# Six row blocks turned by TensorE, lists turned two experts ahead, and a new order of stage 1, in a fused attention and expert kernel

## The chip, the cores and the metric

The kernel runs on one core of a Trainium2 chip. The metric is the time of one execution on the device in microseconds (us), lower is better. The kernel before took 283.99 us (median of three runs, 281.12 to 286.87). A core has TensorE (PE; its weight loads are listed as PEld), VectorE (DVE), ScalarE (ACT), GpSimd (POOL) and SyncE (SP), and 16 DMA engines which all DMA issues share. [...]

## The reference

```python
# q, k, v: (2 batches, 8 heads, 768 tokens, 64)
state = gamma * state + outer(k[t], v[t])       # per batch and head, gamma fixed for a head
y[t]  = scale * q[t] @ state                    # linear attention with decay
x     = y of all heads side by side             # (2, 768, 512)
logits = x @ w_gate                             # 8 experts
local  = sigmoid(x @ w_local)
e[s] = argmax(logits[s]) if s == 0 or local[s] < 0.5 else e[s-1]     # runs along the tokens
out[s] = softmax(logits[s])[e[s]] * (relu(x[s] @ w1[e[s]]) @ w2[e[s]])
```

Each of the 1536 tokens goes to one expert, `w1` is 512 x 1024 and `w2` 1024 x 512 in float32, so the weights of all eight experts are 33.6 MB.

## The kernel before

**Stage 1** is the attention, in 12 chunks of 128 tokens (6 per batch). For chunk c the rows of `k`, `v` and (for two chunks at once) `q` are loaded (`lk`, `lv`, `lq`), POOL scales `k` and `q` by powers of gamma (`dk`, `dq`, lines 370 and 361), TensorE turns them so that the head dimension is on the partitions (`tk`, `tq`, lines 426 and 399) and ACT or DVE copies the result out of PSUM (`ek`, `eq`, line 379). Then come the scores (`sc`, line 441), their causal mask on DVE (`mk`, line 446), the part of `y` from the state (`in`, line 458) and the part from the chunk itself (`re`, line 467), and the state's update (`st`, line 502; `sn` copies it out). `xh` on ACT and `xl` on DVE write `y` as the sum of two float16 tiles, `xT` (lines 476 and 480), from which the router's logits are computed (`lo`, lines 517 and 522).

**The rows.** `xT` has features on the partitions. The experts gather tokens as rows from DRAM, so each chunk's `xT` must be turned back: before, this is one DMA transpose for each chunk (`xd`, line 485), then a DMA that writes the rows to the DRAM tensor `xs` (`xs`, line 491).

**Routing** is done for groups of three chunks (`ch`, `kr`, `ke`, `tr`, `ca`, `tc`, `oh`, `co`, `pl`, `es`, `fi`, `ad`): the choice, the carried choice along the tokens by a scan, and the place of each token in its expert's list. After the first six chunks early lists of experts 0 and 1 are made from the tokens known so far (`ep`, `eg`), their rows gathered (line 655) and turned by DMA (`xx`, line 723). With them the first halves of experts 0 and 1 can be computed in stage 1: these are the 48 **fillers** `f` (per expert 16 pieces of the first product, line 750, and 8 of the second, line 809; `ra` and `rv` are ACT's and DVE's parts of the relu). When all groups are done, `rank`, `lists` and `experts` make the final lists and `ga` gathers from them.

**Weights** are loaded in pieces of 512 KB (`W`, line 151), each split into float16 high (`wh` on ACT, line 161) and low parts (`wl` on DVE, line 169). Nine staging buffers hold pieces; the split units of two experts fit at a time. Sixteen pieces (experts 0 and 1) are loaded in stage 1 and four more at its end.

**Order.** Everything in stage 1 is issued in the order of the text `ORDER`: a token such as `xd.3` calls the function for chunk 3, and each engine executes its own instructions in that order. All loads, DMA transposes and `xs` writes are issued from SP, one after another: an issue that waits holds up what stands behind it there. **Stage 2** follows: a loop over the experts computes the second halves of experts 0 and 1 and then the other six, loading weights as it goes; `transposed` (line 716) turns the gathered lists of the next expert and starts the next gather. Below, "stage 2" begins with the first product of expert 0's second half.

Of the kernel before, what the change touches and what calls it, by code (L numbers as in the profile page):

```python
# [43 lines left out]
ORDER = """
warm.10 zero lc.0 lk.0.0 lq.0.0 lk.0.1 lq.0.1 in.0 dk.0.p.0 lc.2 tk.0.t.0 dq.0.p.0 ek.0.a.0 lc.1 lv.0 dk.0.p.1
tqh.0.0.t dq.0.p.1 tk.0.x.1 eqh.0.0.v lg ek.0.a.1 lk.1 cast tqh.0.1.t eqh.0.1.v lv.1 st.0 setup sc.0 sn.0.a lk.2
dk.1.p mk.0.0 lq.2 mk.0.1 tk.1.t re.0 ek.1.a lv.2 dk.2.p sc.1 xh.0 lk.3 xl.0 dq.2.p mk.1.0 lo.0 xd.0 st.1 mk.1.1 in.1
lv.3 sn.1.a dk.3.p tq.2.0.t lk.4 re.1 eq.2.0.a xs.0 tq.2.1.t xh.1 W tk.2.x xl.1 eq.2.1.a st.2 ek.2.a dk.4.p xd.1 lo.1
sn.2.a sc.2 lq.4 in.2 wh.a mk.2.0 wh.a mk.2.1 xs.1 tk.3.t wl re.2 W ek.3.a wl dq.4.p sc.3 xh.2 W xl.2 st.3 mk.3.0 xd.2
lo.2 mk.3.1 sn.3.a wh.a in.3 lv.4 ch.0 wh.a ch.0 kr.0 wl wh.a lk.5 re.3 ke.0 ch.0 ch.0 ch.0 wh.a wl xs.2 tr.0 xh.3 wl  # L50
tq.4.0.t W tq.4.1.x ca.0 eq.4.0.a st.4 eq.4.1.a xl.3 dk.5.p tc.0 W sn.4.a tk.4.t oh.0 co.0 ek.4.a wl lo.3 xd.3 sc.4
pl.0 es.0 wh.a pl.0 lv.5 pl.0 wh.a in.4 mk.4.0 wh.a lk.6 mk.4.1 wh.a fi.0 re.4 ad.0 wl xs.3 wl lq.6 tk.5.t xh.4 wl
ek.5.a xl.4 dk.6.p sc.5 W wl lo.4 mk.5.0 W in.5 mk.5.1 dq.6.p tk.6.t xd.4 re.5 ek.6.v wh.a lv.6 wh.a wl tq.6.0.t xh.5
wl lk.7 tq.6.1.x eq.6.0.a xl.5 eq.6.1.a lo.5 wh.a xs.4 sc.6 ch.1 wh.a W ch.1 ch.1 kr.1 ch.1 wl st.6 ke.1 W ch.1 mk.6.0
dk.7.p tr.1 sn.6.a in.6 ca.1 xd.5 tk.7.t mk.6.1 wh.a tc.1 lv.7 wh.a oh.1 wl co.1 ek.7.a re.6 pl.1 es.1 lk.8 wh.a pl.1
pl.1 wh.a tot sc.7 xh.6 xs.5 ev wl W xl.6 fi.1 st.7 ad.1 ep wl lo.6 sn.7.a lq.8 in.7 wl eg.0 mk.7.0 mk.7.1 eg.1 W wh.a
wl re.7 wh.a dk.8.p xd.6 xh.7 dq.8.p xx.0.0 tk.8.t xl.7 ek.8.a lo.7 xx.1.0 wh.a wh.a wl xs.6 tq.8.0.t tq.8.1.x wl
eq.8.0.a W f eq.8.1.a wl f in.8 wl lv.8 f lk.9 f wh.a f W f wh.a wl f ra wl st.8 xd.7 rv f sn.8.a dk.9.p ra f W rv f
tk.9.t wh.a f lv.9 ek.9.a wl f wh.a f xs.7 ra wl f lk.10 rv wh.a f wh.a f wl ra lq.10 st.9 wl f rv sn.9.a sc.8 W
dk.10.p f mk.8.0 W mk.8.1 tk.10.x dq.10.p f ek.10.a lv.10 re.8 wh.a wh.a lk.11 wl sc.9 xh.8 wl wh.a lv.11 tq.10.0.x  # L60
xl.8 wh.a f mk.9.0 eq.10.0.a xd.8 lo.8 mk.9.1 in.9 ch.2 ch.2 kr.2 ch.2 ch.2 dk.11.p re.9 ke.2 xs.8 ch.2 wl xh.9 tr.2
tq.10.1.x ca.2 st.10 eq.10.1.a sc.10 xl.9 sn.10.a wl xd.9 tc.2 mk.10.0 lo.9 oh.2 in.10 mk.10.1 co.2 xs.9 re.10 pl.2
es.2 pl.2 pl.2 tk.11.x xh.10 fi.2 xl.10 ek.11.a f ad.2 xd.10 lo.10 sc.11 in.11 mk.11.0 mk.11.1 xs.10 f re.11 f xh.11
xl.11 f xd.11 lo.11 hd.0 f ch.3 f ch.3 kr.3 ch.3 f ch.3 ke.3 ch.3 tr.3 f ca.3 xs.11 ra f f rv tc.3 f oh.3 co.3 f pl.3
es.3 ra f pl.3 pl.3 tot f f rank fi.3 f ad.3 lists ra experts ga rest W prob W W ga rv rv f xx.0.1 f f W f ra f rv ga
f f f f ga f f f hd.1 ga
"""
# [954 lines left out]
```

## Time and profile before

| | |
|---|---|
| median of three runs | 283.99 us (281.12 to 286.87) |
| the profiled execution | 283.82 us, of which the span of the trace is 282.0 us |
| PE busy | 236.5 us (84%) |
| DVE, ACT, POOL busy | 160.6 us (57%), 127.2 us (45%), 63.7 us (23%) |
| DMA | 61.76 MB, mean 219 GB/s; 58156 of 80339 packets under 512 B |

The page divides the span into 40 equal slices and gives for each the busy share of every engine in tenths, TensorE's granted clock and what the DMA engines moved. A busy engine is no bound by itself: what counts is which wait ends last in a stage. Times "from the start" are from the start of the span. The DMA share of a short stretch can read over 1.

### The profile page before, as it was taken

What the parts mean: (1) busy time and instruction counts of PE and PEld (TensorE: products, weight loads), DVE (VectorE), ACT (ScalarE), POOL (GpSimd) and SP (SyncE); (2) the same over time, 40 slices, a digit from 0 to 9 for tenths busy, and PEclk for the clock granted to TensorE, in tenths of its full rate; (3) what the DMA queues carried; (4) which work ended last, traced back from release to release, by engine and by line L of the source; (5) the groups of instructions that cost most, each with busy time, mean ns of one, the idle gap of its engine ahead of it and who ended that gap; (6) DMA issues with size and microseconds to landing.
All of it is one profiled execution on the core that took longest, in us unless ns stands there. A gap on an engine that the chain in (4) does not pass through costs nothing. (4 is left out here: it accounts for less than half of the span.)

```text
span 282.0 us, 6110 instructions
## 1 busy us (share of the span) xinstructions
PE 236.5 (84%) x2372; PEld 177.8 (63%) x2372; DVE 160.6 (57%) x379; ACT 127.2 (45%) x260; POOL 63.7 (23%) x69
## 2 busy tenths in 40 slices
PE   7688797694796799737899899999999999999950
PEld 3576575483584686533857684785875966949740
DVE  0535985875045774860379786586595683932300
ACT  2243572444153532201189666476584765813210
...
GB/s 171 216 198 284 276 261 301 253 265 236 190 273 271 201 101 88 77 227 241 335 304 186 367 372 321 406 274 392 293 304 351 264 262 68 24 11 40 0 47 7
DMA packets 80339, 61.76 MB, mean 219 GB/s; under 512 B 58156, under 2 KB 64556, under 8 KB 80304
## 3 DMA queue, kind: packets, MB, share of 16 engines
...
q8 instruction: 20, 0.33, 0.5%
...
## 5 line engine op out<-in xcount | busy, mean ns | idle before, releaser
L169 DVE SCALAR_TENSOR_TENSOR lo<-stg,hi 128x512 f16<-128x512 f32 x128 | 83.8, 691 | 32.8 <-ACT hi L161 29.1
L750 PE MATMUL h<-xx,hi 128*128 128x128 f16 (+5 forms) x640 | 81.2, 248 | 11.4 <-DMA xx<-xg 5.8
L161 ACT ACTIVATE hi<-stg 128x512 f16<-128x512 f32 x128 | 73.5, 620 | 26.3 <-DMA stg<-in_moe_w_dram 26.1
L750 PE MATMUL h<-xx,lo 128*128 128x128 f16 (+5 forms) x320 | 74.6, 248 | 0.0
L750 PEld LDWEIGHTS <-hi 128*128 128x128 f16 x640 | 57.7, 101 | 16.4 <-DVE hl L770 5.7
L839 POOL DMA_INDIRECT out_dram<-ob,sidx x16 | 19.2, 1202 | 100.0 <-ACT ob L838 39.2
L809 PE MATMUL o<-hi,hh 128*128 128x512 f16 (+3 forms) x104 | 39.7, 382 | 0.0
L809 PE MATMUL o<-lo,hh 128*128 128x512 f16 (+3 forms) x104 | 39.4, 379 | 0.0
L809 PE MATMUL o<-hi,hl 128*128 128x512 f16 (+3 forms) x104 | 39.4, 379 | 0.0
L809 PEld LDWEIGHTS <-hh 128*128 128x128 f16 (+3 forms) x240 | 24.4, 104 | 21.2 <-issue 0.3
L770 DVE SCALAR_TENSOR_TENSOR hl<-h,hh 128x256 f16<-128x256 f32 (+3 forms) x48 | 19.4, 406 | 25.7 <-ACT hh L769 15.4
L750 PEld LDWEIGHTS <-lo 128*128 128x128 f16 x320 | 32.4, 101 | 0.6
L769 ACT ACTIVATE hh<-h 128x256 f16<-128x256 f32 (+3 forms) x48 | 17.8, 371 | 31.1 <-PE h L750 30.9
L370 POOL TENSOR_TENSOR ks<-ink,ct 128x512 f32<-128x512 f32 (+1 forms) x13 | 12.7, 978 | 48.3 <-DMA ink<-in_k_dram 48.3
L655 POOL DMA_INDIRECT xg<-xs,gidx x16 | 16.8, 1052 | 28.3 <-DMA xx<-xg 10.3
L809 PEld LDWEIGHTS <-hl 128*128 128x128 f16 (+3 forms) x120 | 12.4, 104 | 12.0 <-issue 0.3
L446 DVE TENSOR_TENSOR am<-sc,ct 128x512 f32<-128x512 f32 x24 | 15.6, 682 | 6.6 <-PE sc L441 6.6
L838 ACT ACTIVATE ob<-o,ptr 128x512 f32<-128x512 f32 (+3 forms) x11 | 7.6, 687 | 24.2 <-issue 16.6
L441 PE MATMUL sc<-qT,kT 64*128 64x128 f32 x192 | 14.9, 297 | 2.6 <-ACT kT L379 2.5
L467 PE MATMUL y<-am,inv 128*64 128x128 f32 x192 | 15.5, 304 | 0.0
L441 PEld LDWEIGHTS sc<-qT,kT 64*128 64x128 f32 x192 | 12.5, 199 | 4.2 <-ACT kT L379 3.0
L361 POOL TENSOR_TENSOR qs<-inq,ct 128x1024 f32<-128x1024 f32 (+1 forms) x7 | 12.1, 1730 | 11.2 <-DMA inq<-in_q_dram 11.2
...
## 6 DMA issues: line engine op xcount, KB each, us to landing
...
```

What stands on the lines that cost most here:

```text
L161: nc.scalar.activation(hi, stg, AF.Copy, scale=2.0**SW)
L169: nc.vector.scalar_tensor_tensor(lo, stg, 2.0**SW, hi, ALU.mult, ALU.subtract)
L370: eng.tensor_tensor(T["ks", c][:, hs], src, tb.unsqueeze(2).to_broadcast([P, n, D]), ALU.mult)
L441: nc.tensor.matmul(scs[j][:, p, :], lhsT=kT[r, p, :], rhs=qT[r, p, :], start=True, stop=True)
L446: nc.vector.tensor_tensor(T["am", c][j], T["sc", c][j], mask_.unsqueeze(1).to_broadcast([P, NP, P]), ALU.mult)
L467: nc.tensor.matmul(y, lhsT=T["v", c][:, hd, :], rhs=am[j][:, p, :], start=(c % NCH == 0 and p == 0), stop=(p == NP - 1), skip_group_check= ...
L655: nc.gpsimd.indirect_dma_start(out=xg, out_offset=None, in_=xs[:top, :], in_offset=bass.IndirectOffsetOnAxis(ap=ix[:, hf * E + e : hf * E ...
L750: nc.tensor.matmul(ps[:, pair_ * P : pair_ * P + n_], lhsT=a[:, kk, fs], rhs=xx[:, b_, kk, :n_], start=(n == 0 and pair_ == 0), stop=(n == ...
L769: lambda: nc.scalar.activation(hh, ps, AF.Relu),
L770: lambda: nc.vector.scalar_tensor_tensor(hl, ps, 0.0, hh, ALU.max, ALU.subtract),
L809: nc.tensor.matmul(po, lhsT=a[:, f, :m], rhs=b_[:, f, cols], start=(f == 0 and n == 0), stop=(f == KF - 1 and n == 2))
L839: nc.gpsimd.indirect_dma_start(out=out[:, :], out_offset=bass.IndirectOffsetOnAxis(ap=LST["sidx"][:m, at_ : at_ + 1], axis=0), in_=ob[:m], ...
```

## The change

1. Rows of chunks 0, 1, 2, 3, 5 and 7 are turned by eight float16 transposes on TensorE into one PSUM bank (`xt`) and copied out by ACT or DVE (`xr`); chunks 4, 6, 8, 9, 10 and 11 keep the DMA transpose.
2. In stage 2 the lists are turned two experts ahead, and the tile for them has three buffers and not two.
3. `ORDER` is another one: more weight pieces stand early, the early lists' DMA transposes late, and the fillers after nearly all of the attention.

```diff
-warm.10 zero lc.0 lk.0.0 lq.0.0 lk.0.1 lq.0.1 in.0 dk.0.p.0 lc.2 tk.0.t.0 dq.0.p.0 ek.0.a.0 lc.1 lv.0 dk.0.p.1
...
-wl re.7 wh.a dk.8.p xd.6 xh.7 dq.8.p xx.0.0 tk.8.t xl.7 ek.8.a lo.7 xx.1.0 wh.a wh.a wl xs.6 tq.8.0.t tq.8.1.x wl
...
+lk.0.0 warm.10 zero lk.0.1 lc.0 lc.2 lv.0 lc.1 in.0 lq.0.0 lq.0.1 lk.1 dk.0.p.0 lv.1 dk.0.p.1 tk.0.t.0 lv.2 cast
+ek.0.a.0 lg tk.0.x.1 ek.0.a.1 lk.2 st.0 lq.2 W sn.0.a dq.0.p.0 W W dq.0.p.1 tqh.0.0.t W W eqh.0.0.v dk.1.p tqh.0.1.x
...
+pl.3 pl.3 tot ra f rank fi.3 f experts f rv W f ad.3 lists W f ra W ga rest W f prob f f f rv f f hd.0 f f ga xx.0.1
+f f ra f rv f f f ra f rv f ga f f f ra rv f f f f ra rv f ga f f f f f ga f hd.1
...
+        def x_transpose(c, b):
+            pool, tag = BANKS[b]
+            tr = pool.tile([P, 2, KD, P], F16, tag=tag, name="xt")
+            for a in range(2):
+                for kk in range(KD):
+                    nc.tensor.transpose(tr[:, a, kk, :], T["xT", c][:, a, kk, :], id16)
+            T["xt", c] = tr
+
+        def x_rows(c, eng):
+            T["xr", c] = tp.tile([P, 2 * DM], F16, tag="xr", name=f"xr{c}")
+            evac(eng, T["xr", c], T.pop(("xt", c)).rearrange("t a k f -> t (a k f)"))
...
-                XX[e] = mp[0].tile([P, 2, KD, CAP], F16, tag="xx", name=f"xx{e}", bufs=2)
+                XX[e] = mp[0].tile([P, 2, KD, CAP], F16, tag="xx", name=f"xx{e}", bufs=3)
...
-            else:
-                transposed(FEW, 0)
-                transposed(FEW, 1)
+            transposed(e + 2, 0)
+            transposed(e + 2, 1)
...
-            if e + 1 < E:
-                transposed(e + 1, 0)
-                transposed(e + 1, 1)
+            if e + 2 < E:
+                transposed(e + 2, 0)
+                transposed(e + 2, 1)
```

The names of the PSUM banks are gathered in a table `BANKS`; the bank that was "z" is now called "s", and no step uses the scores' pool under that letter any more. The line numbers of the changed kernel are some 14 higher behind the new functions.

**SP's queue at the early lists.** `xx` are the early lists (experts 0 and 1), `xr` and `xs` the rows of a chunk, `stg` a weight piece, `ink`, `inq` and `inv` the inputs. Before:

```order
L485 DMA_TRANSPOSE xr_898<-xT_827 128x8x128
L723 DMA_TRANSPOSE xx_0_904<-xg_0_877 128x8x128
L723 DMA_TRANSPOSE xx_0_922<-xg_0_881 128x8x128
L491 DMA xs<-xr_898 128x1024
L151 DMA stg_3_941<-in_moe_w_dram 128x1024
L352 DMA inv_970<-in_v_dram 128x8x64
L352 DMA ink_978<-in_k_dram 128x8x64
```

Now:

```order
L352 DMA ink_1064<-in_k_dram 128x8x64
L487 DMA_TRANSPOSE xr_1075<-xT_872 128x8x128
L505 DMA xs<-xr_1082 128x1024
L505 DMA xs<-xr_1075 128x1024
L737 DMA_TRANSPOSE xx_0_1161<-xg_0_1084 128x8x128
L737 DMA_TRANSPOSE xx_0_1196<-xg_0_1098 128x8x128
L487 DMA_TRANSPOSE xr_1222<-xT_1109 128x8x128
L487 DMA_TRANSPOSE xr_1243<-xT_1203 128x8x128
L352 DMA inv_1273<-in_v_dram 128x8x64
```

The two list transposes stood ahead of `v` of chunk 8, `k` of chunk 9 and all loads after them; now they stand behind the last load of `k` (chunk 10's, since chunk 11's is issued before it), and of the inputs only `v` of chunk 11 is behind them, after the DMA transposes of chunks 8 and 9.

**TensorE at the scores of chunk 8.** Line 441 (now 443) is the scores, 809 a filler, 502 (now 516) the state, 426 a turn of `k`, 531 the logits. Before:

```order
L502 MATMUL st_739<-inv_1063,ks_1030 64x64 x8
L809 MATMUL o<-hi_575,hh_0_943 128x512
L809 MATMUL o<-lo_576,hh_0_943 128x512
L809 MATMUL o<-hi_575,hl_0_944 128x512
L441 MATMUL sc<-qT_933,kT_912 128x128 x8
L809 LDWEIGHTS hh_0_943
L426 MATMUL tr<-ct,ks_1141 128x128 x4
```

Now:

```order
L469 MATMUL y<-am_0_969,inv_676 64x128
L469 MATMUL y<-am_1_970,inv_676 64x128
L443 MATMUL sc<-qT_755,kT_990 128x128 x8
L516 MATMUL st_764<-inv_868,ks_957 64x64 x8
L531 LDWEIGHTS xT_1029
L531 MATMUL lgb<-w_68,xT_1029 128x18
```

Fillers stood between the attention's steps here; now there is attention alone, and the fillers begin between the scores and the last product of chunk 11: 45 of the 48 stand behind chunk 11's logits, where 24 stood before.

**ACT at the first chunks.** `hi` is the split of a weight piece, `xT` the copy of `y`, `xr` the new copy of turned rows, `kT` and `qT` the copies of turned inputs. Before:

```order
L379 ACTIVATE kT_216<-tr 128x512
L476 ACTIVATE xT_234<-y 128x512
L379 ACTIVATE sbd_102<-st_171 128x256
L379 ACTIVATE qT_280<-tr 128x512
L476 ACTIVATE xT_298<-y 128x512
```

Now:

```order
L379 ACTIVATE kT_239<-tr 128x512
L161 ACTIVATE hi_278<-stg_0_168 128x512
L478 ACTIVATE xT_289<-y 128x512
L379 ACTIVATE kT_294<-tr 128x512
L161 ACTIVATE hi_278<-stg_1_173 128x512
L379 ACTIVATE qT_301<-tr 128x512
L379 ACTIVATE xr_340<-xt 128x1024
L161 ACTIVATE hi_278<-stg_2_175 128x512 x2
L478 ACTIVATE xT_375<-y 128x512
```

Splits of weight pieces now stand ahead of the copies of chunks 0 and 1, so ACT waits for a weight piece before it copies `y` of the first chunk.

## Rows read from the trace of the kernel before

**Rows 1.** Busy time by stretch: start:end, length, PE, PEld, DVE, ACT, POOL, granted clock, DMA share, GB/s.
```profile
10.00:58.00 48.00, 37.74 (x534) 30.91 (x530) 31.43 (x74) 22.47 (x44) 14.29 (x16) 0.94 1.14 259
17.00:19.00 2.00, 1.41 (x20) 1.06 (x18) 0.00 (x0) 0.54 (x1) 0.71 (x1) 1.00 1.30 89
36.00:37.00 1.00, 1.00 (x23) 0.90 (x20) 0.43 (x3) 0.88 (x3) 0.63 (x1) 1.00 1.00 404
58.00:89.00 31.00, 21.99 (x256) 18.78 (x256) 14.28 (x27) 12.25 (x25) 6.62 (x5) 0.76 1.06 245
102.00:104.00 2.00, 2.00 (x40) 1.73 (x40) 1.50 (x4) 0.00 (x0) 0.13 (x1) 1.00 0.72 139
112.00:135.00 23.00, 14.03 (x147) 9.69 (x146) 10.90 (x56) 3.25 (x8) 5.37 (x8) 0.85 0.78 173
135.00:270.00 135.00, 133.81 (x1124) 98.46 (x1124) 86.66 (x179) 78.89 (x166) 28.19 (x24) 1.00 0.79 238
```

**Rows 2.** TensorE in order of time: start, length, line, operands, count.
```profile
10.25 1.16 PE L441 MATMUL sc<-qT,kT 64*128 64x128 f32 x16
...
16.09 1.09 PE L458 MATMUL y<-qT,sbd 64*64 64x128 f32 x16
...
18.36 1.09 PE L467 MATMUL y<-am,inv 128*64 128x128 f32 x16
19.38 0.66 PE L399 MATMUL tr<-ct,qs 128*128 128x128 f32 x4
...
20.40 0.69 PE L502 MATMUL st<-inv,ks 128*64 128x64 f32 x16
21.02 0.26 PE L517 MATMUL lgb<-w,xT 128*128 128x18 f16 x4
...
51.80 0.33 PE L574 MATMUL lgb<-c,old 128*1 128x128 f16 x3
...
58.20 2.08 PE L441 MATMUL sc<-qT,kT 64*128 64x128 f32 x16
```

**Rows 3.** TensorE later; in brackets idle time before, and what ended it.
```profile
88.71 1.16 PE L441 MATMUL sc<-qT,kT 64*128 64x128 f32 x16
...
106.47 1.16 PE L441 MATMUL sc<-qT,kT 64*128 64x128 f32 x16
...
111.67 0.25 PE L517 MATMUL lgb<-w,xT 128*128 128x18 f16 x4
...
128.34 0.38 PE L809 MATMUL o<-hi,hh 128*128 128x512 f16 x1
...
128.99 0.38 PE L809 MATMUL o<-hi,hh 128*128 128x512 f16 x1
...
135.17 0.28 PE L750 MATMUL h<-xx,hi 128*128 128x128 f16 x2 [2.78 <-DMA xx<-xg]
...
135.34 0.28 PE L750 MATMUL h<-xx,hi 128*128 128x128 f16 x2
...
158.18 0.38 PE L750 MATMUL h<-xx,hi 128*128 128x256 f16 x2 [1.02 <-DMA xx<-xg]
```

**Rows 4.** SP's queue in order of time, the same columns.
```profile
20.16 0.43 SPq L151 DMA_DIRECT2D stg<-in_moe_w_dram  x1
...
60.50 0.56 SPq L151 DMA_DIRECT2D stg<-in_moe_w_dram  x1
...
70.44 2.96 SPq L723 DMA_TRANSPOSE xx<-xg  x2
...
75.09 0.53 SPq L352 DMA_DIRECT2D ink<-in_k_dram  x1
```

**Rows 5.** POOL in order of time: the scaling of chunk 8's k.
```profile
81.19 1.04 POOL L370 TENSOR_TENSOR ks<-ink,ct 128x512 f32<-128x512 f32 x1 [11.71 <-DMA ink<-in_k_dram]
```

**Rows 6.** Groups of one form: count, busy us, mean ns, idle before, releaser.
```profile
L379 ACT ACTIVATE kT<-tr 128x512 f32<-128x512 f32 x10 | 5.9, 590 | 6.9 <-PE tr L426 6.9
```

**Rows 7.** DVE in order of time: the final lists are written.
```profile
119.16 0.17 DVE L229 TENSOR_SCALAR gidx<-tabr 128x16 int32<-128x16 f32 x1
```

More of the change, by code (lines that the diff above doesn't have):

```diff
@@ L44 @@
 ORDER = """
-warm.10 zero lc.0 lk.0.0 lq.0.0 lk.0.1 lq.0.1 in.0 dk.0.p.0 lc.2 tk.0.t.0 dq.0.p.0 ek.0.a.0 lc.1 lv.0 dk.0.p.1
[L46 to L54, printed above, removed]
@@ L55 @@
-dk.7.p tr.1 sn.6.a in.6 ca.1 xd.5 tk.7.t mk.6.1 wh.a tc.1 lv.7 wh.a oh.1 wl co.1 ek.7.a re.6 pl.1 es.1 lk.8 wh.a pl.1
-pl.1 wh.a tot sc.7 xh.6 xs.5 ev wl W xl.6 fi.1 st.7 ad.1 ep wl lo.6 sn.7.a lq.8 in.7 wl eg.0 mk.7.0 mk.7.1 eg.1 W wh.a
-wl re.7 wh.a dk.8.p xd.6 xh.7 dq.8.p xx.0.0 tk.8.t xl.7 ek.8.a lo.7 xx.1.0 wh.a wh.a wl xs.6 tq.8.0.t tq.8.1.x wl
-eq.8.0.a W f eq.8.1.a wl f in.8 wl lv.8 f lk.9 f wh.a f W f wh.a wl f ra wl st.8 xd.7 rv f sn.8.a dk.9.p ra f W rv f
-tk.9.t wh.a f lv.9 ek.9.a wl f wh.a f xs.7 ra wl f lk.10 rv wh.a f wh.a f wl ra lq.10 st.9 wl f rv sn.9.a sc.8 W
@@ L60 @@
[L60 to L64, printed above, removed]
@@ L65 @@
-es.3 ra f pl.3 pl.3 tot f f rank fi.3 f ad.3 lists ra experts ga rest W prob W W ga rv rv f xx.0.1 f f W f ra f rv ga
-f f f f ga f f f hd.1 ga
+lk.0.0 warm.10 zero lk.0.1 lc.0 lc.2 lv.0 lc.1 in.0 lq.0.0 lq.0.1 lk.1 dk.0.p.0 lv.1 dk.0.p.1 tk.0.t.0 lv.2 cast
+ek.0.a.0 lg tk.0.x.1 ek.0.a.1 lk.2 st.0 lq.2 W sn.0.a dq.0.p.0 W W dq.0.p.1 tqh.0.0.t W W eqh.0.0.v dk.1.p tqh.0.1.x
+lq.4 W eqh.0.1.v st.1 lk.3 W sc.0 sn.1.a W W setup tk.1.t ek.1.a mk.0.1 dk.2.p mk.0.0 sc.1 lk.4 dq.2.p re.0 mk.1.1
+mk.1.0 tk.2.t lv.3 wh.a st.2 xh.0 wl lq.6 ek.2.a tq.2.0.x xl.0 wh.a tq.2.1.t eq.2.0.v wh.a lo.0 wl xt.0.x eq.2.1.a
@@ new lines @@
+in.1 wl xr.0.a W sc.2 sn.2.a xs.0 wh.a wh.a re.1 mk.2.0 wh.a mk.2.1 wh.a lv.4 wl xh.1 wh.a W xl.1 dq.4.p wh.a xt.1.t
+wh.a in.2 xr.1.v wh.a lq.8 wh.a tq.4.0.x dk.3.p xs.1 re.2 eq.4.0.a wl lk.5 tk.3.t xh.2 lv.5 wl lo.1 ek.3.a tq.4.1.x
+xl.2 W wh.a sc.3 wl eq.4.1.a wh.a lo.2 mk.3.1 xt.2.t wh.a mk.3.0 in.3 wh.a ch.0 wh.a wh.a ch.0 kr.0 ch.0 dk.4.p ke.0
+st.3 re.3 sn.3.a ch.0 lk.6 ch.0 wl tk.4.x lv.6 xh.3 dq.6.p W tr.0 xl.3 ek.4.a ca.0 lo.3 wh.a xt.3.x lq.10 xr.2.a wl
+tc.0 sc.4 oh.0 wl wh.a xs.2 co.0 mk.4.0 W in.4 es.0 mk.4.1 wh.a pl.0 pl.0 st.4 wl wh.a re.4 pl.0 sn.4.a wl tq.6.0.t
@@ new lines @@
+lv.7 xh.4 wl W fi.0 eq.6.0.a xl.4 xr.3.a tq.6.1.t dk.5.p ad.0 lo.4 eq.6.1.v in.5 xs.3 dq.8.p lk.7 tk.5.t ek.5.a wh.a
+sc.5 wl wh.a dk.6.p W tq.8.0.t mk.5.1 tq.8.1.x mk.5.0 eq.8.0.a st.6 lk.8 eq.8.1.a wl re.5 wl sn.6.a wh.a wl tk.6.t
+lv.10 xh.5 wl ek.6.a xl.5 wh.a sc.6 dq.10.p xd.4 xt.5.t mk.6.1 lo.5 mk.6.0 in.6 wh.a ch.1 re.6 wh.a ch.1 ch.1 kr.1
+lv.8 ch.1 xh.6 ch.1 wl tr.1 ke.1 xl.6 wh.a ca.1 lo.6 in.7 xr.5.a wl tc.1 wh.a xs.5 dk.7.p oh.1 co.1 pl.1 pl.1 tk.7.t
+lk.9 pl.1 wh.a st.7 ek.7.a es.1 wh.a fi.1 sn.7.v dk.8.p sc.7 ad.1 ep tk.8.t lk.11 mk.7.0 tq.10.0.x ek.8.a mk.7.1 tot
@@ new lines @@
+eq.10.0.a tq.10.1.t xs.4 ev wl re.7 eq.10.1.a wl sc.8 wl lv.9 xh.7 xl.7 st.8 mk.8.1 dk.9.p lo.7 sn.8.a mk.8.0 in.8
+dk.11.p lk.10 xt.7.t xd.6 tk.9.x xr.7.a eg.1 wl re.8 ek.9.v xs.7 eg.0 wl st.9 xh.8 tk.11.t xl.8 sn.9.a sc.9 ek.11.a wl
+dk.10.p in.9 mk.9.1 mk.9.0 xs.6 lo.8 tk.10.t wl xx.1.0 st.10 ch.2 ek.10.a re.9 sn.10.a ch.2 wl xx.0.0 kr.2 ch.2 xh.9
+ch.2 sc.10 wl ke.2 xd.8 xl.9 mk.10.0 lo.9 in.10 xd.9 mk.10.1 ch.2 wl tr.2 re.10 ca.2 sc.11 lv.11 wl xh.10 xl.10 xs.8
+tc.2 mk.11.1 lo.10 in.11 mk.11.0 xs.9 oh.2 wl co.2 f pl.2 es.2 pl.2 re.11 pl.2 xd.10 fi.2 xh.11 f xl.11 f ad.2 lo.11
@@ L67 @@
+xd.11 f ch.3 f ra kr.3 ch.3 ch.3 f ch.3 ke.3 ch.3 rv tr.3 f ca.3 xs.10 f ra f rv tc.3 f oh.3 co.3 xs.11 f pl.3 es.3 f
+pl.3 pl.3 tot ra f rank fi.3 f experts f rv W f ad.3 lists W f ra W ga rest f W f prob f f f rv f f hd.0 f f ga xx.0.1
+f f ra f rv f f f ra f rv f ga f f f ra rv f f f f ra rv f ga f f f f f ga f hd.1
 """
@@ L383, in evac @@
                 nc.vector.tensor_scalar(dst, src, scale, None, ALU.mult)
+        BANKS = {"x": (ps_1, "xt"), "t": (ps_tr, "tr"), "y": (ps_1, "y"), "s": (ps_st, "st")}
         def bank(b):
-            pool, tag = {"s": (ps_sc, "sc"), "x": (ps_1, "xt"), "t": (ps_tr, "tr"), "y": (ps_1, "y"), "z": (ps_st, "st")}[b]
+            pool, tag = BANKS[b]
             return pool.tile([P, NP, P], F32, tag=tag, name="tr")
@@ L488, in x_turn @@
             T["xr", c] = xr
+        def x_transpose(c, b):
+            pool, tag = BANKS[b]
+            tr = pool.tile([P, 2, KD, P], F16, tag=tag, name="xt")
[6 more added lines that the diff above has]
+            evac(eng, T["xr", c], T.pop(("xt", c)).rearrange("t a k f -> t (a k f)"))
         def x_store(c):
@@ L791, in down @@
                 if part is not None:
-                    to = bank("yz"[part]).rearrange("p a b -> p (a b)")[:, : DM // 2]
+                    to = bank("ys"[part]).rearrange("p a b -> p (a b)")[:, : DM // 2]
                     PO[e, hf] = PO.get((e, hf), []) + [to]
@@ L875, in moe_kernel @@
             "tq": q_transpose, "eq": q_evac, "tk": k_transpose, "ek": k_evac,
-            "sc": scores, "mk": mask, "in": inter, "re": retain, "xh": x_hi, "xl": x_lo, "xd": x_turn, "xs": x_store,
+            "sc": scores, "mk": mask, "in": inter, "re": retain, "xh": x_hi, "xl": x_lo, "xd": x_turn, "xt": x_transpose, "xr": x_rows, "xs": x_store,
             "st": state, "sn": snapshot, "lo": logits,
```

## Prediction

> **What bounds the kernel now.** I read the busy time by stretch first, because the kernel has two stages and a mean hides them. [...]
>
> Chunk 0's scores start at 10.25, chunk 7's at 58.20 [rows 2]: (58.20 - 10.25) / 7 = 6.85 us for each chunk. Chunk 8's start at 88.71 and chunk 11's at 106.47 [rows 3]: 17.76 / 3 = 5.92 us. The step from 7 to 8 takes 30.51 us, 23.7 more than the first pace. SP's queue shows why: the two DMA transposes of the early lists are issued only at 70.44, and chunk 9's `k` behind them only at 75.09 [rows 4]; POOL meanwhile idles 11.71 us for chunk 8's `k` and scales it at 81.19 [rows 5]. Fillers are put into this hole: 16 pieces of the first product and one of the second. A first piece is six matmuls, of which three take 0.17 us (135.17 to 135.34), so 0.33 us; a second piece takes 128.99 - 128.34 = 0.65 us [rows 3]. That is 5.9 us of work in a hole of 23.7 us.
>
> The chain of waits of the profile covers only the last store and says nothing of this; the landmarks have to carry the argument.
>
> **The change part by part.** The sum is made against the profiled execution: 283.82 us, 282.0 of them the span; the median is 283.99, so no correction is needed.
>
> *Early lists behind the loads.* The hole after chunk 7 goes: the list transposes now stand behind the loads of `k` of all chunks. I therefore let the first pace hold for all eleven steps. It is bounded from below by TensorE's own steps: scores 1.16, state part 1.09, own part 1.09, turns of `q` and of `k` 0.66 each, state 0.69, logits twice 0.26 [rows 2], together 5.9 us.
>
> *Turns on TensorE.* 48 float16 transposes of 128x128 are added. The nearest row is the routing's product with the float16 identity, three in 0.33 us [rows 2], a matmul of the same size. Three of the first product's take 0.17 us from start to start [rows 3], so each costs 0.06, and eight with the drain of the last 0.6 us: 3.6 us for six chunks. From above, float32 turns are four in 0.66 us [rows 2], so at most 1.3 us a chunk, 7.9 us in all. I take 3.6, and half of it, 1.8 us, on the path, since TensorE idles 10 of the 48 us from 10 to 58 [rows 1]. The copy out of PSUM is twice the size of a `kT` copy, 0.59 us [rows 6], so 1.2 us, five on ACT and one on DVE. ACT is busy 22.47 of 48 us there [rows 1]; I cost these at nothing. If ACT stands at a weight split, the copy and the bank behind it are late: a rival below.
> [...]
>
> *DMA.* One turn alone takes a share of 0.72 over 2 us, 1.4 us of all 16 engines; among loads, throughput fell to 89 GB/s for 2 us [rows 1]. Five of the six removed turns (chunks 0 to 3 and 5) lay ahead of chunk 7's scores: 7.2 us of DMA time freed. Against that the new order has all 16 weight pieces ahead of these scores; before, eleven were issued from 20.16 to 60.50 [rows 4]. Five more pieces of 0.524 MB cost 1.3 us each at 404 GB/s or 2.0 at 259 [rows 1], 6.5 to 10 us. I take it as even: pace 6.85 unchanged. The bounds are 6.2 us (the 5.9 plus six chunks' 0.6 spread over twelve, no waits left) and 7.85 us (the weights' 6.5 to 10 us, say 7, over seven steps, with nothing given back by the turns).
>
> *Start.* `q` of chunk 0 now stands behind 0.59 MB more (constants, `v`, `k`): 2.3 us at 259 GB/s [rows 1]. Chunk 0's scores at 12.5.
>
> *Chunk 11 to stage 2.* From chunk 11's scores (106.47) to its logits (111.67) pass 5.2 us, with three second pieces in between (2.0 us); now three first pieces (1.0): 4.2 us. From the logits to stage 2 pass 23.5 us [rows 3], and here two things must end. The final lists are written at 119.16, 7.5 us behind the logits [rows 7]; the last thing before stage 2 was a wait of 2.78 us for the turned list of expert 0, which let TensorE start at 135.17 [rows 3], 16.0 us behind the lists. And TensorE must do its fillers: 32 of them stand behind the lists now (16 first, 16 second, 5.3 + 10.4 = 15.7 us), so 7.5 + 15.7 = 23.2 us. Before there were 24 fillers behind the logits, now 45. Twenty-one fillers more cost nothing, because the wait for lists and transfers is what they cover; if the lists came faster, the fillers would set the end. I keep 23.5.
>
> *Two experts ahead.* In stage 2 TensorE waited for a turned list once, 1.02 us before expert 2 at 158.18 [rows 3]. That goes. The two extra transposes stand ahead of weight pieces on SP, hidden while TensorE has 133.81 of 135 us of work [rows 1]; if the weights came late they would cost 1.4 us each. I take 1.0 off.
>
> **Sum.** Chunk 11's scores: 12.5 + 11 x 6.85 + 1.8 = 89.7. Logits 93.9, stage 2 at 117.4, against 135.17: 17.8 us earlier, and 1.0 in stage 2. 283.8 - 18.8 = **265 us**.
>
> **The rivals.**
> 1. *TensorE's own pace.* With the turns out of the DMA queues the waits vanish and 6.2 us a chunk holds, from a start at 10.25: scores 11 at 78.5, stage 2 at 106.2, 254 us. For it: 89 to 106 ran at 5.92 with fillers. Against it: then the loads had landed; at 10 to 58 the DMA share was 1.14 [rows 1].
> 2. *Weights first.* The splits stand ahead of the copies of `y` on ACT, and each waits for its weight piece; 16 pieces go through the first seven chunks and the pace is 7.85: 11 us more, 276 us. For it: the DMA engines were full already [rows 1].
> 3. *The hole only moves.* The early lists still stop SP. Behind them are the DMA turns of chunks 8 and 9 and `v` of chunk 11; if chunk 11 stands still for all that passed on SP from the last weight piece to the list transposes (70.44 - 60.50 = 9.9 us, at most) and for both transposes (2.96 us) [rows 4], 278 us. The change would then not do what its order says. Against it: `v` of chunk 11 is used three chunks later.
> [...]
> [...]
>
> **How the numbers follow.** About 2%, 5.7 us, is what a measurement of this kernel tells from no change. Forecast 265: 0.52. Rival 1, 254: 0.13. Rival 2, 276: 0.18. Rival 3, 278: 0.08. Rival 4, 291: 0.09. The range reaches from rival 1 to the upper bound of the pace and rival 3, 254 to 278. Faster by over 2% means under 278.3: the forecast, rival 1 and a good half of rivals 2 and 3, 0.80. Within 2%: the rest of these two and the mild form of rival 4, 0.13. Slower: 0.07.
>
> **What would show it.** Chunk 7's and 8's scores should be one pace apart; chunk 11's scores near 90, stage 2 near 117, and the span behind it as long as before (282.0 - 135.17 = 146.8) or 1 us less. A row of float16 turns should read about 0.6 us for eight. [...] The forecast is wrong if stage 2 itself grows, by weights that come late, or if the wait from the final lists to the first turned list is more than 16 us.

## The result and the profile after

The changed kernel takes 263.15 us, the median of four runs (259.19 to 268.3), against 283.0 for the kernel before beside it: a ratio of 0.922, with a 95% interval of 0.907 to 0.936. Ratios leave disturbed runs of either kernel out, so they are not the quotient of the medians. The forecast was 265.0. The profiled execution took 261.32 us, 259.5 of them the span, and all views of after are of it.

Busy time by stretch, with the columns of [rows 1]: the first seven chunks, the step from there to chunk 7, the rest of the attention with the fillers, and stage 2.

```profile
10.00:58.00 48.00, 40.22 (x558) 33.19 (x558) 33.90 (x72) 31.02 (x56) 17.95 (x15) 0.94 1.03 302
58.00:65.00 7.00, 5.58 (x64) 4.27 (x60) 5.45 (x16) 4.52 (x8) 3.29 (x5) 0.67 1.20 232
65.00:116.00 51.00, 47.56 (x641) 36.86 (x640) 35.01 (x116) 12.97 (x27) 12.98 (x17) 0.98 0.85 198
116.00:251.50 135.50, 135.10 (x1137) 99.56 (x1134) 85.47 (x179) 80.04 (x168) 26.43 (x24) 1.00 0.81 234
```

Stage 2 is what it was: 135.10 us of TensorE in 135.50, against 133.81 in 135 [rows 1]. The hole of 58 to 89 is gone: chunk 8's scores come 4.95 us behind chunk 7's, where 30.51 us passed. The line to look at twice is the first: from 10 to 58 us the DMA engines moved 302 GB/s at a share of 1.03, where they moved 259 at 1.14 [rows 1]. That is 14.5 MB in place of 12.4, in a tenth less DMA time.

TensorE in order of time (start, length, line, operands, count; in brackets the idle time before): scores of chunks 0, 6, 7, 8 and 11, one group of float16 turns, a turn of the last `q`, chunk 11's logits, and the last filler with the first product of stage 2.

```profile
9.98 2.11 PE L415 MATMUL tr<-ct,qs 128*128 128x128 f32 x8 [2.63 <-POOL qs L361]
...
13.28 2.08 PE L443 MATMUL sc<-qT,kT 64*128 64x128 f32 x16
...
21.71 0.61 PE L497 MATMUL xt<-c,xT 128*128 128x128 f16 x8 [0.16 <-DVE qT L381]
...
54.56 1.16 PE L443 MATMUL sc<-qT,kT 64*128 64x128 f32 x16 [1.44 <-ACT kT L379]
...
65.39 2.01 PE L443 MATMUL sc<-qT,kT 64*128 64x128 f32 x16
...
67.82 0.60 PE L401 MATMUL tr<-ct,qs 128*128 128x128 f32 x4
...
70.34 1.16 PE L443 MATMUL sc<-qT,kT 64*128 64x128 f32 x16
...
85.65 1.16 PE L443 MATMUL sc<-qT,kT 64*128 64x128 f32 x16
...
90.96 0.25 PE L531 MATMUL lgb<-w,xT 128*128 128x18 f16 x4
...
115.66 0.38 PE L823 MATMUL o<-hi,hl 128*128 128x512 f16 x1
115.88 0.28 PE L764 MATMUL h<-xx,hi 128*128 128x128 f16 x2
```

| landmark on TensorE, us | before | forecast | after |
|---|---|---|---|
| chunk 0's scores | 10.25 | 12.5 | 13.28 |
| chunk 6's scores | 50.62 | | 54.56 |
| chunk 7's scores | 58.20 | | 65.39 |
| chunk 8's scores | 88.71 | | 70.34 |
| chunk 11's scores | 106.47 | 89.7 | 85.65 |
| chunk 11's logits | 111.67 | 93.9 | 90.96 |
| stage 2 starts | 135.17 | 117.4 | 115.88 |
| from there to the end of the span | 146.8 | 145.8 | 143.6 |

The last filler and the first product of stage 2 touch (115.66 + 0.38 against 115.88: they overlap by 0.16), so no turned list is waited for, where 2.78 us were [rows 3].

SP's queue, the same columns, from the last loads of `k` to `v` of chunk 11.

```profile
59.76 3.67 SPq L487 DMA_TRANSPOSE xr<-xT  x1
...
71.78 0.37 SPq L352 DMA_DIRECT2D ink<-in_k_dram  x1
...
78.19 3.35 SPq L737 DMA_TRANSPOSE xx<-xg  x2
...
84.41 0.53 SPq L352 DMA_DIRECT2D inv<-in_v_dram  x1
```

The last load of `k` is issued at 71.78. Before, it was issued at 88.78, a row that the prediction did not use:

```profile
88.78 0.89 SPq L352 DMA_DIRECT2D ink<-in_k_dram  x1
```

Ahead of it stood ten DMA transposes then, eight of chunks and two of lists; now one, chunk 4's at 59.76. The moment of this load is what the experiments came to turn on.

### The profile page after: what moved, and what is told of

Read it like the earlier page. It is cut to its first block, busy times and chain, and to the rows that moved or that the text cites. A ratio compares the mean times of both kernels' runs of the same rounds, so it can differ in the third digit from the quotient of the medians.

```text
span 259.5 us, 6195 instructions
## 1 busy us (share of the span) xinstructions
PE 234.5 (90%) x2420; PEld 176.3 (68%) x2420; DVE 161.0 (62%) x383; ACT 131.1 (51%) x262; POOL 64.3 (25%) x69
## 5 line engine op out<-in xcount | busy, mean ns | idle before, releaser
L169 DVE SCALAR_TENSOR_TENSOR lo<-stg,hi 128x512 f16<-128x512 f32 x128 | 85.4, 701 | 16.0 <-ACT hi L161 13.2
L764 PE MATMUL h<-xx,hi 128*128 128x128 f16 (+5 forms) x640 | 77.8, 242 | 0.0
L764 PE MATMUL h<-xx,lo 128*128 128x128 f16 (+5 forms) x320 | 71.7, 242 | 0.0
L764 PEld LDWEIGHTS <-hi 128*128 128x128 f16 x640 | 55.9, 98 | 3.8 <-issue 0.3
L853 POOL DMA_INDIRECT out_dram<-ob,sidx x16 | 18.4, 1148 | 93.4 <-ACT ob L852 26.4
L764 PEld LDWEIGHTS <-lo 128*128 128x128 f16 x320 | 31.3, 98 | 0.6
L823 PEld LDWEIGHTS <-hl 128*128 128x128 f16 (+3 forms) x120 | 12.4, 103 | 13.3 <-DVE hl L784 1.6
L370 POOL TENSOR_TENSOR ks<-ink,ct 128x512 f32<-128x512 f32 (+1 forms) x13 | 15.1, 1171 | 24.9 <-DMA ink<-in_k_dram 20.9
L443 PE MATMUL sc<-qT,kT 64*128 64x128 f32 x192 | 15.7, 309 | 2.9 <-ACT kT L379 2.9
L443 PEld LDWEIGHTS sc<-qT,kT 64*128 64x128 f32 x192 | 13.3, 210 | 4.9 <-ACT kT L379 3.9
L379 ACT ACTIVATE kT<-tr 128x512 f32<-128x512 f32 (+1 forms) x12 | 6.7, 561 | 15.1 <-PE tr L428 15.0
```

Of the source, the lines that this page charges most:

```text
L169: nc.vector.scalar_tensor_tensor(lo, stg, 2.0**SW, hi, ALU.mult, ALU.subtract)
L370: eng.tensor_tensor(T["ks", c][:, hs], src, tb.unsqueeze(2).to_broadcast([P, n, D]), ALU.mult)
L443: nc.tensor.matmul(scs[j][:, p, :], lhsT=kT[r, p, :], rhs=qT[r, p, :], start=True, stop=True)
L764: nc.tensor.matmul(ps[:, pair_ * P : pair_ * P + n_], lhsT=a[:, kk, fs], rhs=xx[:, b_, kk, :n_], start=(n == 0 and pair_ == 0), stop=(n == ...
L823: nc.tensor.matmul(po, lhsT=a[:, f, :m], rhs=b_[:, f, cols], start=(f == 0 and n == 0), stop=(f == KF - 1 and n == 2))
L853: nc.gpsimd.indirect_dma_start(out=out[:, :], out_offset=bass.IndirectOffsetOnAxis(ap=LST["sidx"][:m, at_ : at_ + 1], axis=0), in_=ob[:m], ...
```

## The experiments

A ratio is to the kernel before on the same chip, with its 95% interval. ORDER's letters: `xd` is the DMA transpose of a chunk's rows, `xt` and `xr` the turn on TensorE and its copy, `xx` a list transpose, `lk`, `lq`, `lv`, `lc` loads, `W` a weight piece, `f`, `ra`, `rv` the fillers and their copies.

**e1: the prediction's main step alone.** The kernel before, with the list transposes behind the last `lv`, and the fillers where the changed kernel has them.

```diff
-dk.8.p xd.6 xh.7 dq.8.p xx.0.0 tk.8.t xl.7 ek.8.a lo.7 xx.1.0 wh.a
+dk.8.p xd.6 xh.7 dq.8.p tk.8.t xl.7 ek.8.a lo.7 wh.a
...
+lv.11 xx.0.0 xx.1.0
```

> The kernel before with one thing moved: the two DMA transposes of the early lists stand on SP behind the last input load (v of chunk 11), and the fillers, which need them, stand where the changed kernel has them; all turns stay with the DMA engines, weights and inputs stay in the old order, lists are turned one expert ahead. Theory A (mine: the hole of 23.7 us after chunk 7 is the change's main term): chunk 7's and 8's scores under 10 us apart, stage 2 starts near 112 to 118, 259 to 267 us. Theory B (the six turns taken from the DMA queues are the main term): the loads stay slow, 276 us or more. Theory C (the earlier weights are): 276 us or more, since they stay where they were.

278.88 us, 0.985 [0.976, 0.993], as theories B and C said and not A. The hole stays. TensorE from chunk 7's scores to chunk 8's:

```profile
59.54 1.16 PE L441 MATMUL sc<-qT,kT 64*128 64x128 f32 x16 [0.39 <-ACT kT L379]
...
68.48 0.66 PE L426 MATMUL tr<-ct,ks 128*128 128x128 f32 x4 [2.86 <-POOL ks L370]
...
73.48 1.97 PE L458 MATMUL y<-qT,sbd 64*64 64x128 f32 x16 [0.71 <-ACT qT L379]
...
79.01 1.12 PE L502 MATMUL st<-inv,ks 128*64 128x64 f32 x16 [3.55 <-DMA inv<-in_v_dram]
...
86.11 2.08 PE L441 MATMUL sc<-qT,kT 64*128 64x128 f32 x16
```

From 59.54 to 86.11 are 26.6 us, without a filler or a list transpose in them. TensorE waits for `k`, `q` and `v` in turn. The loads are as late as before, with no list ahead of them (`v` of chunk 8 is issued at 74.31, before at 74.60): the DMA engines are full (a share of 1.09 from 60 to 87 us, columns of [rows 1]), and SP's queue itself stands behind a DMA turn. Issued at 62.58, its rows can be stored only at 73.00, and the loads wait behind that store.

```profile
60.00:87.00 27.00, 13.41 (x156) 10.80 (x154) 13.59 (x21) 10.83 (x21) 6.98 (x6) 0.68 1.09 250
```
```profile
62.58 4.45 SPq L485 DMA_TRANSPOSE xr<-xT  x1
73.00 0.33 SPq L491 DMA_DIRECT2D xs<-xr  x1
```

SP's waits tell the same (line, what it waited for: us in total, times, the longest one). In the kernel before, from 60 to 79 us, SP did stand at the list transposes, for the gather of their rows; in e1, from 60 to 75, it stood for the turn about as long:

```profile
SPq L723 <- DMA xg<-xs,gidx: 6.4, 1, 6.4
```
```profile
SPq L491 <- DMA xr<-xT: 7.2, 2, 6.0
```

In the old order, chunk 8's scores stand behind the state of chunk 8, the turn of chunk 9's `k` and the state of chunk 9, so they need the loads of two chunks, with weight pieces between them. The list transposes were two transfers among many. (The scaling at 81.19 in [rows 5] is that of chunk 9's `k`; chunk 8's was scaled at 65.50.)

```profile
65.50 1.05 POOL L370 TENSOR_TENSOR ks<-ink,ct 128x512 f32<-128x512 f32 x1
```

**e2: the turns alone, in the old order** (one list ahead as before).

```diff
-mk.1.0 lo.0 xd.0 st.1 mk.1.1
+mk.1.0 lo.0 xt.0.x xr.0.a st.1 mk.1.1
...
-wl st.8 xd.7 rv f
+wl st.8 xt.7.x xr.7.a rv f
```

> The kernel before with one thing changed: the rows of chunks 0, 1, 2, 3, 5 and 7 are turned by TensorE and copied out by ACT, at the places of their DMA transposes. Theory A: the hole after chunk 7 stays near 30 us and the time falls by at most the freed DMA time ahead of it (five turns of 1.4 us), 276 to 284 us. Theory B: most of the gain is here, 270 us or less.

272.04 us, 0.956 [0.947, 0.965], between the ranges of the two theories: more than half of the gain of the whole change, though 26.4 of the hole's 30.5 us are still there (chunk 7's scores at 53.91, chunk 8's at 80.32). The last load of `k`:

```profile
80.36 1.35 SPq L352 DMA_DIRECT2D ink<-in_k_dram  x1
```

It is 8.42 us earlier than before, and six turns at the 1.4 us of [rows 1] are 8.4.

**e3: the order alone.** The changed kernel with all twelve chunks turned by DMA.

```diff
-xt.0.x eq.2.1.a in.1 wl xr.0.a W
+xd.0 eq.2.1.a in.1 wl W
...
-dq.4.p wh.a xt.1.t wh.a
+dq.4.p wh.a xd.1 wh.a
```

> The changed kernel with its order, but all twelve chunks turned by DMA, each at the place where TensorE turned it. Theory A: the six turns were forecast as even against five weight pieces, 7.2 us of DMA time in the first seven chunks, so 264 to 272 us. Theory B: most of the gain is lost, 277 us or more.

271.73 us, 0.954 [0.944, 0.965]: as much as the turns alone, and at the upper end of theory A's range. The two parts add up: spans of 282.0 before, 271.6 with the turns, 270.9 with the order, 259.5 with both, so the turns save 10.4 in the old order and 11.4 in the new, the order 11.1 and 12.1.

The scores of chunks 7 and 8 in e3:

```profile
73.67 2.08 PE L443 MATMUL sc<-qT,kT 64*128 64x128 f32 x16
...
79.16 1.16 PE L443 MATMUL sc<-qT,kT 64*128 64x128 f32 x16
```

The new order closes the hole by itself, to 5.5 us, with every turn still a DMA. In it chunk 8's scores need no load of chunk 9 any more, and no weight piece stands between the two scores. What the six turns give in this order comes ahead of chunk 7: its scores are at 73.67 with DMA turns and at 65.39 without, 8.3 us earlier.

**e4: lists turned one expert ahead**, in the changed kernel, with two buffers.

```diff
-XX[e] = mp[0].tile([P, 2, KD, CAP], F16, tag="xx", name=f"xx{e}", bufs=3)
+XX[e] = mp[0].tile([P, 2, KD, CAP], F16, tag="xx", name=f"xx{e}", bufs=2)
...
-if e + 2 < E:
-    transposed(e + 2, 0)
+if e + 1 < E:
+    transposed(e + 1, 0)
```

> The changed kernel with the lists turned one expert ahead and two buffers, as before. Theory A: one wait of about 1 us for a turned list comes back in stage 2, 263 to 265 us against 263. Rival: turning two ahead also moves weights, and the part is worth more, 267 us or more; or the two extra transposes ahead of the weights cost, and it is 261 us or less.

265.58 us, 0.939 [0.930, 0.947], which overlaps the change's interval and lies between the expected ranges. From the start of stage 2 (120.1) to the end of the span pass 143.5 us, with the change 143.6, and TensorE waits for no turned list there. The 4 us by which stage 2 starts later lie in stage 1, which is the same program in both; that this is spread between executions is likely, but not shown. Two ahead is worth nothing that can be seen here.

**e5: more turns.** These four left a new theory, D: stage 1 lasts as long as the DMA engines need for all that is issued ahead of the last load of `k`, and each DMA turn there costs 1.4 us. The rival was that a turn costs only through the wait of its store in SP's queue, as at 73.00 in e1. So: the kernel before, with a second DMA turn of chunks 0 to 7 into a tile that nothing reads, and no store behind it.

```diff
             T["xr", c] = xr
+            if c < 8:
+                again = a1.tile([P, 2 * DM], F16, tag="again", name="again")
+                nc.sync.dma_start(
+                    out=again.rearrange("t (k f) -> t k f", f=P), in_=T["xT", c].rearrange("f a k t -> f (a k t)"),
+                    transpose=True,
+                )
```

> The kernel before, in which the DMA turns of chunks 0 to 7 are each issued a second time into a tile that nobody reads (eight extra turns, all ahead of the last load of k). Theory D (stage 1 is bound by the DMA engines' time up to the last load of k, and a turn ahead of it costs 1.4 us): that load is issued at 88.8 + 8 x 1.4 = 100 us, and the time is 290 to 298 us. Theory A (the early lists on SP made the hole): the extra turns fill DMA time that had waits in it anyway, 280 to 287 us.

293.64 us, 1.044 [1.037, 1.050].

```profile
100.26 0.98 SPq L352 DMA_DIRECT2D ink<-in_k_dram  x1
```

The last load of `k` comes 11.48 us later, 1.435 for each turn, and the span grows by 11.3. Eight transfers that nobody waits for delayed the whole kernel.

Whether they did so by the DMA engines' time alone is not shown. A lone turn takes 1.4 us of them [rows 1], but its issue also holds SP's queue, in the kernel before for at least 1.23 us, a load of `k` for at least 0.39 (min/median/max in ns):

```profile
L485 SPq DMA_TRANSPOSE xr<-xT x12: 1231/1246/2802, 15.3 to 111.9; - x12
L352 SPq DMA_DIRECT2D ink<-in_k_dram x13: 386/889/2732, 1.2 to 88.8; - x13
```

No run takes the two apart.

**e6: everything but the rest of the order.** The kernel before with e1's move, e2's turns and the lists two ahead, so that only the earlier weight pieces and the start are missing (its diff is that of e1 and e2).

> The kernel before with the six turns on TensorE, the early lists behind the last input load, the fillers at the end, and two experts ahead: all of the change but the rest of its order (the weights early, the loads' and the copies' new places). Theory D: six turns and two list turns less ahead of the last load of k, 8 x 1.4 = 11.2 us, so it is issued near 77.6 us and the time is 266 to 271 us; what is then missing to 263 is the rest of the order. If the parts only add up as measured one by one (10.8 and 3.9 us): 268 us. Theory A': the rest of the order is worth nothing, 261 to 265 us.

270.07 us, 0.955 [0.947, 0.964], in theory D's range; profiled, the last load of `k` is at 74.25 and the span is 265.3. By the turns alone (eight fewer) it should be at 77.6; 3.3 us of it are not accounted for (the profiled execution, 267.04 us, was itself 3.0 us under the median). By ratio it is no better than e2, whose interval it shares, so the late lists add nothing that can be told.

Over these kernels the span follows the last load of `k`:

| kernel | last load of `k`, us | span, us | difference |
|---|---|---|---|
| e5 | 100.26 | 293.3 | 193.0 |
| before | 88.78 | 282.0 | 193.2 |
| e1 | 86.27 | 278.2 | 191.9 |
| e3 | 82.04 | 270.9 | 188.9 |
| e2 | 80.36 | 271.6 | 191.2 |
| e6 | 74.25 | 265.3 | 191.1 |
| e4 | 74.74 | 263.6 | 188.9 |
| after | 71.78 | 259.5 | 187.7 |

The moment moves by 28 us, the rest by 5.5; the new order has 187.7 to 188.9, the old one 191.1 to 193.2. That both move together does not yet say which of them sets the other; e5 shows it for the old order, e10 below has the answer for the new one.

**e7 and e8: two small moves in the changed kernel.** e7 puts `q` of chunk 0 ahead of the constants and `v`; e8 scales and loads `k` of chunks 7 and 8 earlier.

```diff
-lk.0.0 warm.10 zero lk.0.1 lc.0 lc.2 lv.0 lc.1 in.0 lq.0.0 lq.0.1 lk.1
+lk.0.0 warm.10 zero lk.0.1 lc.0 lq.0.0 lq.0.1 lc.2 lv.0 lc.1 in.0 lk.1
```
```diff
-lq.10 xr.2.a
+lq.10 dk.5.p lk.7 xr.2.a
...
-lv.7 xh.4
+lv.7 dk.6.p lk.8 xh.4
```

> The changed kernel with q of chunk 0 loaded ahead of two pieces of the constants and of v of chunk 0. The start term: chunk 0's scores come 2 us earlier (11 in place of 13.3) and TensorE's idle time of 2.6 us before the turns of q gets shorter, so the granted clock from 10 to 20 us rises from 0.70. Theory D: the first 65 us are paced by the DMA engines, which carry the same bytes, so the time stays at 261 to 265 us. Rival (the start is a chain of its own): 260 us or less.

> The changed kernel with the loads of k of chunks 7 and 8 (and the scaling that frees their buffers) ahead of weight pieces and row stores behind which they stood on SP. Chunk 7's scores came 10.8 us after chunk 6's, with the granted clock at half. If that was SP's queue: k of chunk 7 is issued at 49 in place of 54, chunk 7's scores 3 to 6 us earlier, 257 to 261 us. If the DMA engines' time sets it (theory D): the same bytes, 262 to 265 us.

e7: 261.62 us, 0.930 [0.922, 0.938]; e8: 263.11, 0.934 [0.928, 0.940]. Neither differs from the change by more than the intervals. In e7 chunk 0's scores start at 12.67, since TensorE now waits 2.74 us for `v`: one wait took the place of the other. In e8 `k` of chunk 7 is issued at 48.43 in place of 54.02, and chunk 7's scores start at 67.65, no earlier than 65.39: they did not wait for that load.

**e9 and e10: four weight pieces behind the last `k`.** If DMA time ahead of that load is all that counts, moving 2.1 MB behind it must bring it forward. e10 also turns chunk 4 on TensorE.

```diff
-co.0 mk.4.0 W in.4 es.0
+co.0 mk.4.0 in.4 es.0
...
-dk.11.p lk.10 xt.7.t
+dk.11.p lk.10 W W xt.7.t
...
-sc.6 dq.10.p xd.4 xt.5.t
+sc.6 dq.10.p xt.4.x xr.4.a xt.5.t
```

> The changed kernel with the last four of the sixteen early weight pieces (2.1 MB, the second matrix of expert 1, needed only by the last eight fillers) loaded behind the last load of k, and their splits moved along. Theory D (the DMA engines' work ahead of the last load of k sets stage 1): 2.1 MB at 300 to 400 GB/s are 5 to 7 us, so that load is issued at 65 to 67 us in place of 72, and the time is 256 to 259 us. Rival F (behind 65 us TensorE is the bound already, so an earlier k gains nothing): 262 to 265 us. Rival G (the pieces come too late for the last fillers or crowd the lists' transposes): over 265 us.

> The kernel before this one, with chunk 4 turned by TensorE too, the last DMA turn ahead of the last load of k. Theory D: 1.4 us less than with the weights alone, 254 to 258 us. Rival F: the same as with the weights alone.

e9 took 273.26 us (267.27 to 275.71), over 265 as rival G said; e10 271.5, 0.953 [0.941, 0.964], slower than the change. Theory D failed here. e10's window from 60 to 70 us and its last load of `k`, with the load ahead of it on SP:

```profile
60.00:70.00 10.00, 8.63 (x81) 7.49 (x81) 6.60 (x16) 1.10 (x2) 4.31 (x7) 0.52 0.32 80
```
```profile
71.87 0.37 SPq L352 DMA_DIRECT2D inv<-in_v_dram  x1
72.33 1.94 SPq L352 DMA_DIRECT2D ink<-in_k_dram  x1
```

The load comes no earlier than 71.78, and the DMA engines stand two thirds idle ahead of it. What holds it is TensorE. `v` of chunk 9 stands ahead of it on SP and takes the buffer of `v` of chunk 7 (there are three), so SP waits until chunk 7's own part (line 469) has read that. SP's wait for it from 60 to 79 us, in e10 and then in the change:

```profile
SPq L352 <- PE y L469: 6.5, 1, 6.5
```
```profile
SPq L352 <- PE y L469: 2.8, 1, 2.8
```

So in the new order the last load of `k` follows chunk 7's scores and does not lead them. e10's scores of chunks 6 and 7 and chunk 7's own part:

```profile
53.74 1.16 PE L443 MATMUL sc<-qT,kT 64*128 64x128 f32 x16 [0.69 <-ACT kT L379]
...
66.28 2.08 PE L443 MATMUL sc<-qT,kT 64*128 64x128 f32 x16
...
70.73 1.09 PE L469 MATMUL y<-am,inv 128*64 128x128 f32 x16
```

Between these scores TensorE waits for no load: all its waits, 3.3 us, are for DVE (the mask, the routing's steps, `xT`), and it works at a granted clock of 0.52 from 60 to 70. With four pieces and a turn taken away, chunk 7's scores come no earlier than the change's 65.39. e10's span then ends 196.9 us behind the load, so the table's rule breaks: what was moved is paid for later, when the four pieces stand ahead of `v` of chunk 11, which is issued at 93.78 in place of 84.41.

```profile
PE y L469 <- DMA inv<-in_v_dram: 5.6, 1, 5.6
```

**e11 and e12: the clock.** In the changed kernel the granted clock is 0.67 from 58 to 65. e11 adds 13 products of 128x512 that nothing reads, at four places from 52.2 to 59.0 us; e12 also has e7's start.

```diff
-wl tk.6.t lv.10
+wl tk.6.t kp.5 lv.10
...
+        def keep_dense(n):
+            pool, tag = BANKS["x"]
+            to = pool.tile([P, DM], F32, tag=tag, name="dense")
+            for _ in range(n):
+                nc.tensor.matmul(to, lhsT=id16, rhs=c16[:, :DM], start=True, stop=True)
```

> The changed kernel with 13 products of 128x512 on constants that nobody reads (2.8 us at the full clock), placed where TensorE waited between 53 and 63 us, before the granted clock fell to half there. If the low clock is a cost of its own: the clock stays at the full level, chunk 7's scores come 3 us or more earlier, 258 to 261 us. Theory D (TensorE waits for the loads there anyway): the clock may stay up, but chunk 8's scores and the time do not move, 262 to 266 us.

> The changed kernel with q of chunk 0 first and with the 13 unread products between 53 and 63 us, the two edits after which single runs showed a higher granted clock (0.96 to 0.98). If low clock is what is left to win in the first 70 us, both add up: granted clock over 0.97, 256 to 261 us. Theory D: the loads set it, 261 to 264 us as with q first alone.

e11: 263.86 us, 0.934 [0.924, 0.944]; e12: 262.02, 0.924 [0.916, 0.931]. Both are in theory D's range. The profiled execution of e11 did what was hoped for. From 50 to 70 us, of e11 and of after:

```profile
50.00:70.00 20.00, 18.58 (x261) 13.96 (x261) 16.51 (x44) 12.22 (x22) 7.39 (x8) 1.00 1.11 282
```
```profile
50.00:70.00 20.00, 15.94 (x199) 13.23 (x199) 15.17 (x40) 11.30 (x20) 6.83 (x8) 0.83 1.13 280
```

TensorE did 2.6 us more work, kept a granted clock of 1.00 where the change has 0.83, and reached chunk 7's scores at 63.35, 2.0 us earlier, and the end at 256.6. But the runs of e11 spread from 258.42 to 267.46, and the median is the change's, though the granted clock over the whole run was 0.974 in the mean of e11's four runs and 0.962 in that of the change's. The gain in one execution is not a gain of the kernel; no version here beats the change by more than the intervals.

## Why the forecast held, step by step

The time was right by 1.9 us, in part by luck. In the profiled execution three parts took 7.5 us more than the sum says (the start 0.8, the first seven steps 4.2, the way from chunk 11 to stage 2 2.5) and three took 11.1 less (the last four steps 7.1, the turns' 1.8 on the path, stage 2 with the end 2.2), so that its span of 259.5 is 3.7 under the 263.2 that the sum gives. The reason was half wrong: the largest term was put down to the wrong move.

**The step that failed: "Early lists behind the loads. The hole after chunk 7 goes: the list transposes now stand behind the loads of `k` of all chunks."** The hole went, but not by that. Doing this move alone left 26.6 of 30.5 us of it and gave 1.5% (e1); the new order with every turn a DMA leaves 5.5 (e3). I had read SP's order of issue as the cause, because chunk 9's `k` stands right behind the transposes [rows 4]. SP did wait there, 6.4 us, but with the lists gone it waited 6.0 for the next turn, at a DMA share of 1.09 (1.06 before, from 58 to 89 [rows 1]). In the old order chunk 8's scores also stand behind the loads of chunk 9, with five weight pieces among them, and the `k` for which POOL idled 11.71 us [rows 5] was chunk 9's; the new order has neither there. Which of its moves counts most was not tried alone.

**The step beside it: "DMA. I take it as even."** Up to chunk 6 it came out: 6.88 us a chunk ((54.56 - 13.28) / 6), 6.73 before ((50.62 - 10.25) / 6). But the terms behind it were not right. The freed turns were put at 7.2 us and gave 8.3 by chunk 7's scores (e3) and 10.4 to 11.4 in all (e2, e3). The weights were counted as five pieces more; of the eleven issued by 60.50, the last two came behind chunk 7's scores at 58.20, so seven pieces more stand ahead of these now.

```profile
50.62 1.16 PE L441 MATMUL sc<-qT,kT 64*128 64x128 f32 x16
```
```profile
59.27 0.68 SPq L151 DMA_DIRECT2D stg<-in_moe_w_dram  x1
```

The price of a turn, 0.72 of 2 us, had been read rightly from [rows 1]: in the old order one ahead of the last load of `k` costs 1.4 us (e2, e5). In the new order five of them delay that load by 10.3 (e3 against the change), more than that price.

**Pace.** 6.85 was taken for all eleven steps. Measured: 7.44 to chunk 7 ((65.39 - 13.28) / 7), because the last of these steps, from chunk 6, took 10.83, with the granted clock at 0.67 from 58 to 65. That is close to rival 2's 7.85, but not its mechanism: ACT waited less for weight pieces in the first 60 us than before (now, then before), and four pieces fewer did not bring chunk 7 forward (e10).

```profile
ACT hi L161 <- DMA stg<-in_moe_w_dram: 4.9, 5, 1.6
```
```profile
ACT hi L161 <- DMA stg<-in_moe_w_dram: 13.9, 5, 5.1
```

Then 4.95 to chunk 8 and 5.10 for each of the last three ((85.65 - 70.34) / 3). These are below the "5.9 us of TensorE's own steps" that I called a lower bound. That bound was wrong for these chunks: it gave each a turn of `q`, and the last `q` is turned by 69.4, ahead of chunk 8's scores; and its rows overlap when they follow each other (chunk 7's own part reads 1.09 us, but chunk 8's scores start 1.02 behind it, 69.32 to 70.34). The mean over all eleven, 6.58, lies between rival 1 and the forecast.

**Turns on TensorE.** Forecast 0.6 us for eight, measured 0.61, and 3.9 in all against 3.6. Copies of 1.02 us against 1.2:

```profile
L497 PE MATMUL xt<-c,xT 128*128 128x128 f16 x48 | 3.9, 219 | 1.5 <-ACT xT L478 1.0 <-DVE xT L482 0.3 <-DVE qT L381 0.2
```
```profile
L379 ACT ACTIVATE xr<-xt 128x1024 f16<-128x1024 f16 x5 | 5.1, 1023 | 1.9 <-PE xt L497 1.8
```

The idle time of 1.5 us before them is the wait for the copies of `y`.

**Start.** 12.5 was forecast, 13.28 came, with 2.63 us of idle time before the turn of `q`. The queue it stands in was read rightly.

**Chunk 11 to stage 2.** Logits 5.31 us behind the scores (4.2 forecast), stage 2 24.9 behind the logits (23.5). The lists are written 8.99 us behind the logits and not 7.5:

```profile
99.95 0.17 DVE L229 TENSOR_SCALAR gidx<-tabr 128x16 int32<-128x16 f32 x1
```

Stage 2 starts 15.9 us behind that. The prediction said that the 15.7 us of fillers and the wait of 16.0 would tie; the fillers ended last, as no wait stands before stage 2.

**Two experts ahead.** 1.0 us was taken off for it; e4 shows none. The wait of 1.02 us before expert 2 is gone, but in e4 as well. So is the rest by which stage 2 and the end are shorter, 146.8 to 143.6 us; its cause was not looked for.

**The rivals.** No run shows the 291 us of rival 4. The granted clock is 0.94 from 10 to 58 and 0.98 from 65 to 116; it was low at the start (0.70 from 10 to 20) and in the step before chunk 7 (0.67 from 58 to 65). Rival 3 was wrong: `v` of chunk 11 was not late in the change, but it was in e10, once weight pieces stood ahead of it.

**What stays open.** Which move inside the new order closes the hole; whether a DMA turn costs by the DMA engines' time or by its issue on SP; the 3.3 us of e6; and what the changed kernel would gain if the step from chunk 6 to chunk 7, with its waits for DVE, were shorter. The spread between runs of the changed kernel goes with the granted clock over the whole run (0.975 at 259.19, 0.965 at 261.32, 0.958 at 264.99, 0.950 at 268.3); what sets it from run to run was not found.
